# Batch 0's q in two loads of two heads, on two queues, and a new written order

## The chip, the cores and the metric

The kernel runs on one core of a Trainium2 chip. The metric is the time of one execution on the device in microseconds (us). It was measured in three runs before the change. One further execution was taken by the profiler, and all rows shown come from it.

## The reference

Softmaxed q and k, no score matrix, then a feed-forward part with a product in it. There are 8 batches, 8 heads, 576 tokens and 64 channels per head; the 4608 tokens then pass through widths 512, 1024, 1024 and 512.

```python
q_s = softmax(q, axis=-1)            # over the 64 channels, sum + 1e-9
k_s = softmax(k, axis=2)             # over the 576 tokens, sum + 1e-9
kv  = einsum('bhsd,bhse->bhde', k_s, v)
x   = einsum('bhsd,bhde->bhse', q_s, kv)   # as (4608, 512)
h   = (x @ w1) * (x @ w2) @ w3
out = h @ w_out
```

## The kernel before, in words

All inputs are float32 in memory; products run in float16. The 576 tokens of a head are laid as 64 partitions times 9 token blocks (`NJ`); two groups of four heads fill the 128 partitions. So one buffer of q for a batch is [128, 4 heads, 9 blocks, 64]. The first eight blocks of each batch make a chunk of 512 tokens for the feed-forward part; the ninth blocks of all batches make a last chunk, number 8.

The two last weights are folded first: `w3` (eight row blocks `w3.0` to `w3.7`) is turned on TensorE (`w3t`), evicted (`w3T`), multiplied by `w_out` (`wo.0`, `wo.1`) in two halves (`pf.ft.0`, `pf.ft.1`) and evicted into `W3O`. Until the first weights have landed, TensorE multiplies zeros (`zero.n`).

For each batch b, q goes through these steps in two parts p. Of the batches' q, batch 0's is turned by TensorE, the others' by a transfer.

- `qmx` (maximum, VectorE), `qsub` (subtraction, VectorE or POOL), `qexp` (ScalarE), `qsm` (sum, VectorE), `qeps` (add 1e-9), `qrc` (reciprocal, VectorE), `qn` (product, VectorE or POOL): tiles `qm`, `q`, `eq`, `qr`, `en`, lines 454 to 496.
- `qt` and `qT`: TensorE turns blocks of 128 and they are evicted, or `qd`: SP issues a transfer that turns them (line 517).
- k goes through `kmx`, `cb`, `ksub`, `kexp` (lines 362 to 414); v is cast in `vc`; `kv` and `kv2` make the 64x64 products (lines 420 to 452).
- `xm`, `xt` multiply turned q by `kv2` (line 535), evicted by `xs`, `xts` into the feed-forward's input.
- For a chunk c: `up.1` (w2), evicted by `bs`; `up.0` (w1); `ab` is their product (VectorE, line 677); `down` multiplies by `W3O` (line 684), `os` evicts, `st` stores.

The whole sequence is a written list, `ORDER`. Each engine and each queue executes its own steps in the order of that list. A suffix picks the engine (`/A` ScalarE, `/D` VectorE, `/P` POOL) or, for `zero`, the count. Steps marked `port` wait on each other when they change between VectorE and POOL (`link`). PSUM has eight banks, handed from step to step.

The inputs of batches 0 and 1 and all weights are loaded on POOL's queue, except the step in `EARLY`, which is on SP's. Loads of batches 2 to 7, the turns `qd` and the stores are on SP's queue. The first load on SP's queue that is not early waits for the third last load on POOL's (`GATE = 3`):

```python
gates[[n for n in loads if plan.steps[n]["eng"] == "SP" and n not in EARLY][0]] = [
    n for n in loads if plan.steps[n]["eng"] == "POOL"][-GATE]
```

Parts of q are cut by token blocks:

```python
PARTS = [(0, 4), (4, NJ)]
cut = slice(PARTS[name[2]][0] * D, PARTS[name[2]][1] * D)
```

Of the kernel before, what the change touches and what calls it, by code (L numbers as in the profile page):

```python
# [67 lines left out]
w3t.3 qT.0.8/A W3O.4/A w3T.3/A pf.5.1 W3O.5/A w3.0 w3t.0 w3T.0/A zero.1/1 pf.3.0 pf.3.1 W3O.3/A cb.0
ksub.0.0/D ksub.0.1/D w3.2 pf.0.0 pf.0.1 w3t.2 q.1.0 qmx.1.0 qsub.1.0/D v.0 kexp.0.0 kexp.0.1 kv.0.0 kv.0 w3.1
w3t.1 w3T.2/A pf.2.0 pf.2.1 W3O.0/A kv2.0 xm.0.0 xm.0.1 qexp.1.0 qsm.1.0 w3T.1/A pf.1.0 pf.1.1 qeps.1.0/D  # L70
xs.0.1.0/D qrc.1.0 qn.1.0/D W3O.2/A w2.2 xs.0.1.1/A up.1.0.1.2 xs.0.0.0/A xs.0.0.1/A k.1 kmx.1.0/D cb.1 w1.2
up.1.0.0.2 up.0.0.0.2 W3O.1/A up.0.0.1.2 bs.0.1.2/A ab.0.1.2 bs.0.0.2/A w2.3 up.1.0.1.3 w2.0 up.1.0.1.0
bs.0.1.0/A up.1.0.0.0 up.1.0.0.3 bs.0.0.0/A bs.0.0.3/A w2.1 up.1.0.0.1 ab.0.0.2 ksub.1.0/D bs.0.0.1/D
up.1.0.1.1 w1.0 up.0.0.1.0 up.0.0.0.0 q.1.1 qmx.1.1 bs.0.1.1/A bs.0.1.3/A ab.0.0.0 w1.1 up.0.0.0.1 w1.3
up.0.0.0.3 up.0.0.1.1 up.0.0.1.3 ab.0.1.0 ab.0.0.3 ab.0.0.1 down.0.0 v.1 ab.0.1.3 ksub.1.1/P k.2 qsub.1.1/P
kexp.1.0 kexp.1.1 qexp.1.1 qsm.1.1 vc.1.1/A os.0.0/A vc.1.0/P kv.1.0 kv.1 down.0.1 qeps.1.1/A ab.0.1.1
down.0.2 qrc.1.1 qn.1.1/P kv2.1 kmx.2.1 kmx.2.0 qd.1.0 os.0.1/A q.2 qmx.2.0 qsub.2.0/P xm.1.0 xt.0 qmx.2.1
qsub.2.1/P os.0.2/A xts.0.0/A xs.1.0.1/A xs.1.0.0/A down.0.3 os.0.3/A xts.0.1/A up.1.1.0.0 up.0.1.0.0
bs.1.0.0/A cb.2 ab.1.0.0 ksub.2.0/P st.0.0 up.1.1.0.1 bs.1.0.1/A up.0.1.0.1 up.1.1.0.2 up.0.1.0.2 v.2 qd.1.1
qexp.2.0 xm.1.1 ab.1.0.1 qsm.2.0 bs.1.0.2/A ab.1.0.2 xs.1.1.0/A xs.1.1.1/A vc.2.0/P qexp.2.1 up.1.1.0.3  # L80
up.0.1.0.3 up.1.1.1.0 qeps.2.0/A qrc.2.0 qn.2.0/P st.0.1 q.3 up.0.1.1.0 up.1.1.1.1 qsm.2.1 bs.1.0.3/A ab.1.0.3
bs.1.1.0/A kexp.2.0 qeps.2.1/A qrc.2.1 qn.2.1/P up.0.1.1.1 up.1.1.1.2 up.0.1.1.2 ksub.2.1/P up.1.1.1.3 qmx.3.1
ab.1.1.0 bs.1.1.2/A ab.1.1.2 qmx.3.0 vc.2.1/A bs.1.1.3/A bs.1.1.1/A k.3 kmx.3.1 ab.1.1.1 kexp.2.1 qsub.3.0/P
down.1.0 down.1.1 os.1.0/A os.1.1/A up.0.1.1.3 q.4 qmx.4.0 xt.1 kv.2 xts.1.0/D ab.1.1.3 qexp.3.0 qsub.4.0/P
qsub.3.1/P down.1.2 os.1.2/A qd.2.0 qd.2.1 kv2.2 xm.2.1 xts.1.1/D xs.2.1.0/A xm.2.0 xs.2.0.0/A xs.2.0.1/A
qsm.3.0 xs.2.1.1/A qeps.3.0/A kmx.3.0 qrc.3.0 qn.3.0/P down.1.3 os.1.3/A cb.3 ksub.3.1/P qexp.3.1 qsm.3.1 k.4
st.0.3 v.3 q.5 st.1.0 qd.3.0 up.1.2.0.0 bs.2.0.0/A up.0.2.0.0 up.1.2.0.1 bs.2.0.1/A up.0.2.0.1 up.1.2.0.2
up.0.2.0.2 qexp.4.0 qeps.3.1/A bs.2.0.2/A kexp.3.1 ab.2.0.1 qrc.3.1 ab.2.0.0 ksub.3.0/P kmx.4.1 kexp.3.0
st.1.1 qn.3.1/P st.0.2 st.1.2 qd.3.1 k.5 v.4 qsm.4.0 qeps.4.0/A qmx.4.1 ab.2.0.2 up.1.2.0.3 up.0.2.0.3
up.1.2.0.4 up.0.2.0.4 up.1.2.0.5 up.0.2.0.5 up.1.2.0.6 bs.2.0.5/A bs.2.0.3/A ab.2.0.3 bs.2.0.4/A bs.2.0.6/A  # L90
ab.2.0.5 ab.2.0.4 up.0.2.0.6 ab.2.0.6 up.1.2.0.7 up.0.2.0.7 vc.3.0/A bs.2.0.7/A qmx.5.1 st.1.3 vc.3.1/P v.5
kv.3 ab.2.0.7 down.2.0 kv2.3 xm.3.1 xm.3.0 qsub.4.1/P qexp.4.1 qsm.4.1 xs.3.1.0/D qrc.4.0 os.2.0/A xt.2
xs.3.0.0/A down.2.1 qsub.5.1/P xs.3.0.1/A xs.3.1.1/A down.2.2 os.2.2/A xts.2.1/A kmx.4.0 q.6 qeps.4.1/D st.2.2
qrc.4.1 down.2.3 up.1.3.0.0 cb.4 os.2.3/A bs.3.0.0/A os.2.1/D xts.2.0/A up.0.3.0.0 qn.4.1/P ksub.4.1/P
up.1.3.0.1 qexp.5.1 bs.3.0.1/A vc.4.0/P kmx.5.1 kexp.4.1 ab.3.0.0 ksub.4.0/P kmx.5.0 up.0.3.0.1 up.1.3.0.2
ab.3.0.1 bs.3.0.2/A vc.4.1/A up.0.3.0.2 up.1.3.0.3 up.0.3.0.3 qmx.5.0 ab.3.0.2 cb.5 st.2.3 qsub.5.0/P qd.4.1
kexp.4.0 qsm.5.1 up.1.3.0.4 bs.3.0.4/A up.0.3.0.4 up.1.3.0.5 bs.3.0.3/A bs.3.0.5/A k.6 qn.4.0/P qd.4.0 st.2.0
ab.3.0.3 ab.3.0.4 up.0.3.0.5 ab.3.0.5 up.1.3.0.6 up.0.3.0.6 vc.5.0/A bs.3.0.6/A up.1.3.0.7 bs.3.0.7/A
ksub.5.1/P kexp.5.1 up.0.3.0.7 xt.3 kv.4 ab.3.0.6 qexp.5.0 qeps.5.1/A ksub.5.0/P v.6 ab.3.0.7 down.3.0
down.3.1 kexp.5.0 os.3.0/A k.7 xts.3.0/A os.3.1/A kmx.6.1 kv2.4 xts.3.1/A down.3.2 qrc.5.1 qmx.6.0 xm.4.0  # L100
os.3.2/A q.7 st.2.1 xs.4.0.0/A xm.4.1 xs.4.0.1/A vc.5.1/P kv.5 qsub.6.0/P qn.5.1/P down.3.3 kmx.6.0 cb.6
ksub.6.1/D kv2.5 xs.4.1.1/A xs.4.1.0/A up.1.4.0.0 up.0.4.0.0 bs.4.0.0/A up.1.4.0.1 st.3.0 qd.5.1 v.7 os.3.3/A
st.3.3 st.3.2 vc.6.1/A bs.4.0.1/A up.0.4.0.1 up.1.4.0.2 ksub.6.0/P ab.4.0.0 qsm.5.0 qmx.6.1 up.0.4.0.2
up.1.4.0.3 up.0.4.0.3 bs.4.0.2/A kexp.6.1 bs.4.0.3/D ab.4.0.2 qeps.5.0/A qrc.5.0 ab.4.0.1 qn.5.0/P qd.5.0
ab.4.0.3 up.1.4.0.4 bs.4.0.4/A up.0.4.0.4 up.1.4.0.5 up.0.4.0.5 up.1.4.0.6 bs.4.0.5/D qexp.6.0 ab.4.0.5
qsm.6.0 ab.4.0.4 qeps.6.0/D bs.4.0.6/A up.0.4.0.6 ab.4.0.6 qrc.6.0 qn.6.0/P qsub.6.1/P up.1.4.0.7 bs.4.0.7/A
up.0.4.0.7 ab.4.0.7 down.4.0 down.4.1 down.4.2 os.4.0/A kexp.6.0 qexp.6.1 kmx.7.1 qmx.7.0 st.3.1 qmx.7.1
os.4.1/D os.4.2/A xt.4 xts.4.1/D xts.4.0/A st.4.0 qd.6.0 vc.6.0/P xm.5.0 kv.6 xm.5.1 kv2.6 qsub.7.0/P
xs.5.0.0/A xs.5.0.1/A xs.5.1.1/A down.4.3 os.4.3/A qsub.7.1/P xs.5.1.0/D up.1.5.0.0 up.0.5.0.0 qsm.6.1
qeps.6.1/D qrc.6.1 kmx.7.0 qn.6.1/P bs.5.0.0/D ab.5.0.0 qd.6.1 st.4.1 st.4.2 vc.7.0/A up.1.5.0.1 up.0.5.0.1  # L110
cb.7 up.1.5.0.2 bs.5.0.2/A up.0.5.0.2 ab.5.0.2 bs.5.0.1/A ab.5.0.1 up.1.5.0.3 ksub.7.1/P bs.5.0.3/A qexp.7.1
up.0.5.0.3 up.1.5.0.4 up.0.5.0.4 up.1.5.0.5 bs.5.0.5/A up.0.5.0.5 qexp.7.0 qsm.7.1 qeps.7.1/A ab.5.0.3
ab.5.0.5 bs.5.0.4/D ab.5.0.4 kexp.7.1 up.1.5.0.6 bs.5.0.6/A vc.7.1/P up.0.5.0.6 ab.5.0.6 qrc.7.1 ksub.7.0/P
kexp.7.0 up.1.5.0.7 bs.5.0.7/D up.0.5.0.7 ab.5.0.7 down.5.0 os.5.0/A xt.5 xts.5.0/A xts.5.1/D xm.6.0
xs.6.0.0/D xs.6.0.1/A qn.7.1/P kv.7 xm.6.1 xt.6 kv2.7 qsm.7.0 down.5.1 down.5.2 down.5.3 qeps.7.0/D qrc.7.0
xs.6.1.1/D xts.6.0/D os.5.2/A os.5.1/A xts.6.1/D xs.6.1.0/D qn.7.0/D st.5.0 qd.7.1 up.1.6.0.0 bs.6.0.0/A
up.0.6.0.0 up.1.6.0.1 bs.6.0.1/A ab.6.0.0 up.0.6.0.1 ab.6.0.1 up.1.6.0.2 bs.6.0.2/D os.5.3/A qd.7.0 xm.7.0
# [688 lines left out]
```

## Time and profile before

| | |
|---|---|
| median of 3 runs | 237.85 us (237.82 to 239.56) |
| the profiled execution | 238.41 us, of it 236.6 us from its first to its last instruction (the span) |
| granted TensorE clock | 1.0 |
| TensorE busy | 228.1 us, 96% |
| VectorE, ScalarE, POOL busy | 183.4, 118.8, 110.3 us |
| moved by transfers | 46.84 MB, mean 198 GB/s over the span |

In the profile PE is TensorE's multiplication, PEld its weight loading, DVE VectorE, ACT ScalarE, POOL GpSimd, SP SyncE. A row names line, engine, operation, the tiles written and read, shapes, count; then busy time and the idle time before, with what ended it. Times in the timeline count from the span's start. A matmul that follows another closely is counted with its pipelined end, so TensorE's busy time is not time at its peak. `w<-in_moe_w_dram` at line 294 is a load of w3, w2sb and w1sb those of w2 and w1. A step's name does not stand in a row; it is found by line, tile and place in the order.

### The profile page before, as it was taken

What the parts mean: (1) busy time and instruction counts of PE and PEld (TensorE: products, weight loads), DVE (VectorE), ACT (ScalarE), POOL (GpSimd) and SP (SyncE); (2) the same over time, 40 slices, a digit from 0 to 9 for tenths busy, and PEclk for the clock granted to TensorE, in tenths of its full rate; (3) what the DMA queues carried; (4) which work ended last, traced back from release to release, by engine and by line L of the source; (5) the groups of instructions that cost most, each with busy time, mean ns of one, the idle gap of its engine ahead of it and who ended that gap; (6) DMA issues with size and microseconds to landing.
All of it is one profiled execution on the core that took longest, in us unless ns stands there. A gap on an engine that the chain in (4) does not pass through costs nothing.

```text
span 236.6 us, 4815 instructions
## 1 busy us (share of the span) xinstructions
PE 228.1 (96%) x1930; PEld 120.6 (51%) x1930; DVE 183.4 (77%) x306; ACT 118.8 (50%) x185; POOL 110.3 (47%) x76
## 2 busy tenths in 40 slices
...
GB/s 152 260 275 279 227 285 253 328 184 390 291 393 175 351 282 253 308 402 297 290 312 379 307 146 70 24 142 3 100 178 47 0 3 0 133 9 143 72 44 133
DMA packets 39926, 46.84 MB, mean 198 GB/s; under 512 B 18400, under 2 KB 23776, under 8 KB 39904
## 3 DMA queue, kind: packets, MB, share of 16 engines
...
q8 instruction: 15, 0.25, 0.4%
...
## 4 chain that ended last, share of the span: by engine, by line
PE 81%; DMA 14%; POOL 2%; DVE 1%; issue 1%; ACT 0%; ACTq 0%; DVEq 0%; POOLq 0%
PE pab L662 51%; PE po L684 21%; DMA v<-in_v_dram 5%; DMA w<-in_moe_w_dram 5%; DMA qT<-en 4%; PE po L699 3%; PE pkv L430 2%; PE xm L535 2%; PE pf L334 2%; POOL en L494 1%; DVE qr L476 1%; DVE ab L677 1%; POOL wosb L294 0%; PE xt L535 0%; POOL q L294 0%
## 5 line engine op out<-in xcount | busy, mean ns | idle before, releaser
L662 PE MATMUL pab<-x,w1sb 128*128 128x512 f16 (+1 forms) x320 | 64.9, 336 | 0.0
L662 PE MATMUL pab<-x,w2sb 128*128 128x512 f16 (+1 forms) x320 | 64.9, 336 | 0.0
L677 DVE TENSOR_TENSOR ab<-pab,bsb 128x512 f16<-128x512 f32 x72 | 47.5, 682 | 14.8 <-PE pab L662 13.8
L684 PE MATMUL po<-W3O,ab 128*128 128x512 f16 x256 | 58.5, 379 | 0.0
L217 ACT CAST bsb<-pab 128x512 f16<-128x512 f32 x54 | 30.9, 586 | 50.2 <-PE pab L662 42.9
L662 PEld LDWEIGHTS <-w2sb 128*128 128x128 f16 x352 | 34.3, 98 | 28.5 <-issue 0.2
L662 PEld LDWEIGHTS <-w1sb 128*128 128x128 f16 x352 | 34.3, 98 | 27.9
L684 PEld LDWEIGHTS <-ab 128*128 128x128 f16 x256 | 24.2, 98 | 28.6 <-issue 0.6
L404 POOL TENSOR_TENSOR k<-k,cb 128x1152 f32<-128x1152 f32 x12 | 31.5, 2631 | 10.9 <-DVE k L404 5.8
L217 ACT COPY osb<-po 128x512 f32<-128x512 f32 (+1 forms) x28 | 15.9, 578 | 40.4 <-PE po L684 28.5
L494 POOL TENSOR_TENSOR en<-eq,qr 128x1280 f16<-128x1280 f16 (+1 forms) x12 | 25.9, 2160 | 15.1 <-DVE qr L487 12.1
L463 POOL TENSOR_TENSOR q<-q,qm 128x1280 f32<-128x1280 f32 (+1 forms) x13 | 27.7, 2141 | 8.7 <-DVE qm L458 8.7
L365 DVE TENSOR_REDUCE km<-k 128x128 f32<-128x1152 f32 x14 | 30.4, 2179 | 0.8 <-DMA k<-in_k_dram 0.8
L217 DVE CAST bsb<-pab 128x512 f16<-128x512 f32 x18 | 12.3, 682 | 16.4 <-PE pab L662 16.2
L458 DVE TENSOR_REDUCE qm<-q 128x16 f32<-128x1024 f32 (+1 forms) x16 | 21.3, 1340 | 4.3 <-DMA q<-in_q_dram 4.3
L471 ACT ACTIVATE eq<-q 128x1024 f16<-128x1024 f32 (+1 forms) x16 | 18.7, 1168 | 11.3 <-DVE q L463 7.8
L476 DVE TENSOR_REDUCE qr<-eq 128x16 f32<-128x1024 f16 (+1 forms) x16 | 21.4, 1335 | 0.5 <-ACT eq L471 0.5
L412 ACT ACTIVATE ek<-k 128x1152 f16<-128x1152 f32 x16 | 18.4, 1165 | 6.5 <-POOL k L404 6.3
L334 PE MATMUL pf<-wosb,w3T 128*128 128x512 f16 x64 | 15.0, 379 | 1.5 <-DMA wosb<-in_moe_w_out_dram 1.5
L221 ACT ACTIVATE x<-xm 128x512 f16<-128x512 f32 x24 | 12.7, 606 | 1.4 <-PE xm L535 1.4
L217 DVE COPY osb<-po 128x512 f32<-128x512 f32 (+1 forms) x9 | 5.9, 654 | 6.7 <-PE po L684 2.8
L243 PE MATMUL zero<-zero 128*128 128x512 f16 x28 | 8.9, 460 | 1.5 <-DVE zero L237 1.5
...
## 6 DMA issues: line engine op xcount, KB each, us to landing
...
k<-in_k_dram SPq DMA_DIRECT2D x6, 1152.0 KB, 6.7
q<-in_q_dram SPq DMA_DIRECT2D x6, 1152.0 KB, 8.7
v<-in_v_dram SPq DMA_DIRECT2D x6, 1152.0 KB, 9.2
...
q<-in_q_dram POOLq DMA_DIRECT2D x2, 640.0 KB, 9.7
...
k<-in_k_dram POOLq DMA_DIRECT2D x1, 1152.0 KB, 14.7
```

The lines of the kernel that those rows point to most:

```text
L217: return [(nc.scalar.copy if eng == "ACT" else engine[eng].tensor_copy)(out=out, in_=in_)]
L334: nc.tensor.matmul(st["pf", ft], lhsT=st["w3T", ft][:, gt, :], rhs=wosb[:, gt, :], start=(gt == 0), stop=(gt == N_FT - 1))
L365: dve.tensor_reduce(out=st["km", b][:, two(hp), :], in_=kb[:, two(hp), :, :].rearrange("p h j d -> p h d j"), axis=AX.X, op=ALU.max)
L404: return [engine[eng].tensor_tensor(out=kb[:, two(hp), :, :], in0=kb[:, two(hp), :, :], in1=st["cb", b][:, two(hp), None, :].broadcast_to( ...
L458: dve.tensor_reduce(out=st["qm", b][:, :, j], in_=qb[:, :, j, :], axis=AX.X, op=ALU.max)
L463: return [engine[eng].tensor_tensor(out=qb[:, :, j, :], in0=qb[:, :, j, :], in1=st["qm", b][:, :, j, None].broadcast_to([P, HH, n, D]), op ...
L471: nc.scalar.activation(out=st["eq", b, p], in_=qb[:, :, j, :], func=AF.Exp)
L476: dve.tensor_reduce(out=st["qr", b][:, :, slice(*PARTS[p])], in_=st["eq", b, p], axis=AX.X, op=ALU.add)
L494: return [engine[eng].tensor_tensor(out=st["en", b][:, j, :, :].rearrange("p j h d -> p h j d"), in0=st["eq", b, p], in1=st["qr", b][:, :, ...
L662: nc.tensor.matmul(st["p", one, c, sub, u][:, a * (t1 - t0):(a + 1) * (t1 - t0)], lhsT=w[:, ct, fb * P:(fb + 1) * P], rhs=x()[:, ct, t0:t1 ...
L677: dve.tensor_tensor(out=st["ab", c][:, nf * u:nf * u + nf, t0:t1], in0=cut(st["p", 0, c, sub, u]), in1=cut(st["bsb", c, sub, u]), op=ALU.mult)
L684: nc.tensor.matmul(st["po", c, tb], lhsT=st["ab", c][:, ft, tb * P:(tb + 1) * P], rhs=W3O[:, ft, :], start=(ft == 0), stop=(ft == N_FT - 1))
```

## The change

Batch 0 (`QH = [0]`) has its q cut by head pairs. Each of the two loads takes two heads of each group with all nine blocks, in rows of 2304 bytes (before: rows of 1024 and 1280 bytes). The first is issued on SP's queue, the second on ScalarE's queue, both ahead of everything else there; ScalarE's table load comes right after its issue. All steps of batch 0's q work on 1152 elements of each partition in both parts. The turn by TensorE is cut into four pieces by head pair and block range instead of three.

```diff
-EARLY = [("q", 0, 0)]
+EARLY = [("q", 0, 0), ("q", 0, 1)]
+BYACT = [("q", 0, 1)]
...
+    QH = [0]
...
-            if n == "k":
+            if n == "k" or i in QH:
                 heads = slice(2 * name[2], 2 * name[2] + 2)
...
-            st[name] = (nc.sync if queue == "SP" else g_).dma_start(out=dst, in_=src)
+            st[name] = {"SP": nc.sync, "ACT": nc.scalar, "POOL": g_}[queue].dma_start(out=dst, in_=src)
+            if name in BYACT[-1:]:
+                table()
...
-        load(name, "SP" if name in EARLY else "POOL")
+        load(name, "ACT" if name in BYACT else "SP" if name in EARLY else "POOL")
...
+        def part(p):
+            if b in QH:
+                return slice(2 * p, 2 * p + 2), slice(0, NJ)
+            return slice(0, HH), slice(*PARTS[p])
...
+        def qth(p, j0, j1):
+            st["qtp", b, p, j0] = bank([P, j1 - j0, P], F16, "qtp")
+            for j in range(j0, j1):
+                n = j * NHP + p
+                nc.tensor.transpose(st["qtp", b, p, j0][:, j - j0, :], blocks(st["en", b], n, n + 1),
+                                    ident16)
```

The list `ORDER` is new from its first step to its last. Its opening, and the stretch about batch 1's q:

```diff
-zero.3/3 zero.4/6 q.0.0 qmx.0.0 qsub.0.0/D w3.6 ident w3t.6 w3T.6/D zero.6/3 qexp.0.0 qsm.0.0 w3.7 w3t.7
-w3T.7/A qeps.0.0/A zero.0 q.0.1 qmx.0.1 qsub.0.1/D qexp.0.1 wo.0 pf.7.0 pf.6.0 wo.1 pf.7.1 pf.6.1 qrc.0.0
+zero.6/1 zero.3/1 q.0.0 qmx.0.0 qsub.0.0/D q.0.1 qmx.0.1 ident w3.7 qexp.0.0 qsm.0.0 zero.1/6 zero.5/1 zero.0
+zero.2/1 w3.4 w3t.4 w3T.4/A qsub.0.1/D qexp.0.1 qeps.0.0/D qrc.0.0 qn.0.0/D w3t.7 w3T.7/A wo.0 pf.4.0 qt.0.0.4
+pf.7.0 qsm.0.1 qeps.0.1/D qrc.0.1 qt.0.0.0 w3.6 w3t.6 wo.1 pf.4.1 k.0.0 qn.0.1/D qT.0.0.4/A kmx.0.0 w3T.6/A
...
+ab.0.1.1 qeps.1.1/A qrc.1.1 ksub.1.1/P qn.1.0/P q.2 qmx.2.0 qmx.2.1 down.0.0 os.0.0/A kexp.1.1 down.0.1
+os.0.1/A vc.1.0/P vc.1.1/P kv.1.0 kv.1 kv2.1 down.0.2 os.0.2/A k.2 kmx.2.0 kmx.2.1 xt.0 qd.1.0 xm.1.0 cb.2
+qn.1.1/P down.0.3 st.0.0 xts.0.1/A qsub.2.0/P xs.1.0.0/A xts.0.0/A xs.1.0.1/A up.1.1.0.0 os.0.3/A up.0.1.0.0
+up.1.1.0.1 bs.1.0.0/A ab.1.0.0 qd.1.1 qsub.2.1/P qexp.2.1 ksub.2.0/P qexp.2.0 qsm.2.0 xm.1.1 up.0.1.0.1
```

On POOL's queue the loads now go w3.7, w3.4, wo.0, w3.6, wo.1, k.0.0, k.0.1, w3.5, w3.0, w3.3, w3.2, w3.1, v.0, q.1.0, w2.3, k.1, w2.2, w2.1, w1.2, q.1.1, w1.3, w1.1, w2.0, w1.0, v.1. Before, they went w3.6, w3.7, q.0.1, wo.0, wo.1, w3.4, k.0.1, w3.5, k.0.0, w3.3, w3.0, w3.2, q.1.0, v.0, w3.1, w2.2, k.1, w1.2, w2.3, w2.0, w2.1, w1.0, q.1.1, w1.1, w1.3, v.1. SP's queue goes on with q.2, k.2, the first turn of batch 1, a store and the second turn; before with k.2, the first turn, q.2, a store, v.2 and the second turn. There are 24 multiplications of zeros instead of 28. The functions for a fused exponential (`qexps`, list `FEXP`) are in the diff but the list is empty.

More of the change, by code (lines that the diff above doesn't have):

```diff
@@ L68 @@
[L68 to L117, printed above, removed]
@@ new lines @@
+pf.7.0 qsm.0.1 qeps.0.1/D qrc.0.1 qt.0.0.0 w3.6 w3t.6 wo.1 pf.4.1 k.0.0 qn.0.1/D qT.0.0.4/A kmx.0.0 w3T.6/A
+pf.7.1 W3O.7/A qT.0.0.0/A W3O.4/A k.0.1 kmx.0.1 cb.0 ksub.0.0/D qt.0.1.4 qt.0.1.0 pf.6.0 zero.4/1 w3.5 w3t.5
+qT.0.1.0/A qT.0.1.4/A w3T.5/A pf.6.1 W3O.6/A w3.0 w3t.0 pf.5.0 pf.5.1 w3.3 w3T.0/A pf.0.0 w3t.3 pf.0.1 W3O.5/A
+kexp.0.0 w3.2 w3t.2 w3.1 w3t.1 v.0 q.1.0 w2.3 w3T.3/D pf.3.0 pf.3.1 w3T.1/A ksub.0.1/D kexp.0.1 k.1 W3O.0/A
+kv.0.0 qmx.1.0 kv.0 kv2.0 pf.1.0 pf.1.1 w2.2 w2.1 w3T.2/A W3O.3/A qsub.1.0/D xm.0.1 xm.0.0 xs.0.0.0/D
@@ new lines @@
+bs.2.0.6/A vc.3.0/A kmx.4.1 ab.2.0.5 v.4 st.0.2 ab.2.0.6 qn.3.0/P st.1.2 qd.3.1 st.0.3 vc.4.1/P qn.4.1/P
+qsub.4.0/P kv.3 bs.2.0.7/A ab.2.0.7 down.2.0 kv2.3 xt.2 xts.2.0/A os.2.0/A qd.3.0 cb.4 qmx.5.1 xm.3.1 xm.3.0
+xs.3.0.1/D down.2.1 xts.2.1/A xs.3.1.1/A xs.3.1.0/A qexp.4.0 qsm.4.0 k.5 kmx.5.1 st.1.0 v.5 down.2.2 down.2.3
+q.6 vc.4.0/A xs.3.0.0/A qeps.4.0/A qrc.4.0 os.2.1/A os.2.3/A up.1.3.0.0 up.0.3.0.0 bs.3.0.0/D qmx.5.0 ab.3.0.0
+ksub.4.1/P kmx.5.0 cb.5 qsub.5.1/P qd.4.1 st.1.3 v.6 st.2.1 qn.4.0/P ksub.4.0/P up.1.3.0.1 up.0.3.0.1 os.2.2/A
```

161 lines of the change are left out of this document (118 added, 43 removed).

## The prediction

> **What bounds the kernel now.** I read the shares of the engines first, then TensorE's waits, the stages, the chain that ended last, and the timeline of the first 64 us. From the page and from the view of TensorE's waits:
>
> ```profile
> PE 228.1 (96%) x1930; PEld 120.6 (51%) x1930; DVE 183.4 (77%) x306; ACT 118.8 (50%) x185; POOL 110.3 (47%) x76
> ...
> PE zero L243 <- DVE zero L237: 1.5, 1, 1.5
> PE pf L334 <- DMA wosb<-in_moe_w_out_dram: 1.5, 2, 0.9
> PE xm L535 <- DMA qT<-en: 1.0, 1, 1.0
> PE pkv L430 <- DMA v<-in_v_dram: 0.7, 1, 0.7
> PE w3t L324 <- DMA w<-in_moe_w_dram: 0.7, 2, 0.4
> ```
>
> TensorE is busy for 228.1 of 236.6 us. It waits 5.4 us in all, 3.9 us of that for transfers, and the latest of these waits (1.0, for the turned q of batch 1) is over by 63 us. The stage from 80 to 100 us says the same, and it names the engine that comes second (columns: stretch, length, then busy us and count of PE, PEld, DVE, ACT, POOL, the granted clock, DMA share, GB/s):
>
> ```profile
> 80.00:100.00 20.00, 20.00 (x175) 9.25 (x174) 19.75 (x33) 15.39 (x25) 15.76 (x8) 1.00 1.07 295
> ```
>
> After 63 us TensorE has no wait left to save, so a new order can only lose there. Whatever can be won lies before that: the waits for transfers, and some of the filler matmuls. VectorE has 0.25 us free in 80 to 100 us, so it is the engine that would make TensorE wait first. The transfers are saturated there too (share above 1).
>
> The opening and the first batches, from the chain that ended last (start, length) and the timeline:
>
> ```profile
> 15.97 12.36 DMA v<-in_v_dram
> 34.64 13.99 PE pab L662 x128
> 54.04 8.99 DMA qT<-en
> 63.07 0.41 PE xm L535 x8
> 75.77 0.18 PE xt L535 x8
> 75.96 0.67 PE pkv L430 x72
> 80.84 13.81 PE pab L662 x64
> ...
> 4.62 1.22 DVE L458 TENSOR_REDUCE qm<-q 128x16 f32<-128x1024 f32 x1 [3.13 <-DMA q<-in_q_dram]
> 9.61 1.49 DVE L458 TENSOR_REDUCE qm<-q 128x20 f32<-128x1280 f32 x1 [0.16 <-DMA q<-in_q_dram]
> 12.54 0.25 DVE L487 RECIPROCAL qr<-qr 128x16 f32<-128x16 f32 x1
> 12.82 1.23 DVE L494 TENSOR_TENSOR en<-eq,qr 128x1024 f16<-128x1024 f16 x1
> 15.48 0.18 DVE L483 TENSOR_SCALAR qr<-qr 128x20 f32<-128x20 f32 x1
> 16.01 1.49 DVE L494 TENSOR_TENSOR en<-eq,qr 128x1280 f16<-128x1280 f16 x1
> 12.04 1.89 PE L334 MATMUL pf<-wosb,w3T 128*128 128x512 f16 x8 [0.95 <-DMA wosb<-in_moe_w_out_dram]
> 16.19 0.66 PE L324 MATMUL w3t<-ident,w 128*128 128x128 f16 x8
> 34.48 1.91 PE L662 MATMUL pab<-x,w2sb 128*128 128x256 f16 x16
> 48.45 1.89 PE L684 MATMUL po<-W3O,ab 128*128 128x512 f16 x8
> ```
>
> VectorE works through batch 0's softmax from 4.62 to 17.50 with almost no gap. TensorE starts the first up product at 34.48 and the first down product at 48.45.
>
> **The change part by part: the loads.** The four heads of q were cut by token block (512 KB on SP's queue at once, 640 KB as the third load of POOL's queue). Now each load has two heads and all nine blocks, 576 KB, issued at once on SP and on ACT. The bytes ahead of any other load hardly change. Before wo.0 stood q.0, two blocks of w3, before v.0 seven of w3, wo, k.0, and q.1.0; now v.0 has eight of w3 ahead, and q.1.0 (512 KB) behind it, a block of w3 being 512 KB too. So I let wo.0 land at about 12 (row 12.04) and v.0 at about 28.3 (15.97 + 12.36) as before: no gain. From the list of transfers in the first 10 us (KB, median us to landing):
>
> ```profile
> q<-in_q_dram SPq DMA_DIRECT2D x1, 512.0 KB, 3.9
> q<-in_q_dram POOLq DMA_DIRECT2D x1, 640.0 KB, 6.5
> ```
>
> The first q load landed at 4.6 with hardly another in flight. Let L be the landing of the first half now. Low end: ACT's load does not disturb it, 64 KB more, 4.8. High end: both halves share evenly. From 4.6 to 9.6 (3.07, its issue, plus 6.5) came 640 KB of q and two w3 blocks that are 1 MB in memory, 1.66 MB in 5 us; the missing 640 KB of q.0 then cost 2.0 us, 6.6. Issued in the same instant, they share; I take 5.8, past the middle of that interval. [...]
>
> **VectorE and TensorE up to the first up.** VectorE has the same elements as before in equal halves of 1152, priced between 1.22 and 1.49: 1.35 each. Its order until the first half is done is maximum, subtraction, maximum of the second, sum, subtraction of the second, epsilon 0.18, reciprocal 0.26, product: 6 x 1.35 + 0.44 = 8.55, with gaps 8.8. So en's first half is ready at L + 8.8 = 14.6 (before: 14.05). TensorE's turn of it stands behind pf.4.0, and all other folds stand behind that turn. From there the same kinds of work follow as before from 16.19 to 34.48 (18.29 us): six w3 turns, 18 turns of q, kv, xm. The differences: 0.65 wait for v gone under later folds, two fillers fewer, three fold halves more (12 matmuls). A 512-column matmul is 13.81 / 64 = 0.216. So 18.29 - 0.65 - 0.43 + 2.59 = 19.8, and the first up stands at 34.4, against 34.48. The four fillers saved are no gain by themselves: 23 of 24 now run at the start, where TensorE would wait for w3 anyway.
>
> **Chunk 0.** Up products take 14.0 (row 34.64), so TensorE would be ready for the first down product at 48.4. VectorE is later. Its stretch here, by these rows:
>
> ```profile
> 34.87 1.22 DVE L372 TENSOR_TENSOR kmx<-k 128x1024 f32<-128x1024 f32 x1
> 39.60 0.45 DVE L400 STREAM_TRANSPOSE cb<-mxe 128x256 f32<-128x256 f32 x1
> 42.54 0.69 DVE L217 CAST bsb<-pab 128x512 f16<-128x512 f32 x1
> 43.15 1.48 DVE L458 TENSOR_REDUCE qm<-q 128x20 f32<-128x1280 f32 x1
> 46.97 1.29 DVE L677 TENSOR_TENSOR ab<-pab,bsb 128x512 f16<-128x512 f32 x2 [0.46 <-PE pab L662]
> ```
>
> xm ends at 34.4 - 1.73 = 32.7 and two evictions of 0.69 to 34.1. Then kmx.1.0 and cb.1 5.2, three bs 2.1, qmx.1.1 1.5, qsm.1.0 1.2, a reciprocal 0.25, seven ab 4.5: 14.7, gaps 0.5, end 49.3. The last of them, ab.0.0.0, is what the first down product reads first. In the old order it was done early. So down.0.0 starts at 49.3, +0.85.
>
> **Batch 1's q, the step that decides.** Its normalisation moves from VectorE to POOL, behind two subtractions of k and one of q; and SP's queue, held until the third last load of POOL has landed, now issues q.2 and k.2 ahead of the turn, where it had k.2 alone. The rows (SP's, then those of POOL and of the waits; after them, from the transfers issued in 40 to 50 us):
>
> ```profile
> 44.05 0.39 SPq L294 DMA_DIRECT2D k<-in_k_dram  x1
> 44.48 3.29 SPq L517 DMA_TRANSPOSE qT<-en  x1
> 47.88 0.52 SPq L294 DMA_DIRECT2D q<-in_q_dram  x1
> 42.56 2.62 POOL L404 TENSOR_TENSOR k<-k,cb 128x1152 f32<-128x1152 f32 x1 [5.76 <-DVE k L404]
> 45.15 2.33 POOL L463 TENSOR_TENSOR q<-q,qm 128x1280 f32<-128x1280 f32 x1
> 48.40 1.14 POOL L217 CAST v<-v 128x1152 f16<-128x1152 f32 x1 [0.92 <-DMA v<-in_v_dram]
> 53.05 4.25 DVE L365 TENSOR_REDUCE km<-k 128x128 f32<-128x1152 f32 x2 [0.65 <-DMA k<-in_k_dram]
> ...
> q<-in_q_dram SPq DMA_DIRECT2D x1, 1152.0 KB, 10.4
> qT<-en SPq DMA_TRANSPOSE x1, 9.4
> ```
>
> Before: k.2 issued at 44.05 held VectorE until 53.05, the turn behind it landed at 53.9 (44.48 + 9.4), the next load at 58.3 (47.88 + 10.4). They land in the order of issue, 0.9 for a turn, up to 4.4 for a load of 1.15 MB; at the 295 GB/s of 80 to 100 us a load takes 4.0. The gate opens at the same time, as the bytes through the third last load are the same. POOL's product: cb.1 ends at 39.3, then 2.6 + 2.3 + 2.6 to 46.9, reciprocal at 47.2, product 1.9 (the 2.33 of the 1280-element subtraction, scaled to 1024): 49.1. That is before the loads ahead have landed, so the queue decides, not POOL. Low end: both loads drain by 54 (53.05 plus little), turn at 54.5. High end: q.2 at 53.05, k.2 4.4 later, turn 1.1: 58.5. I take q.2 at 52.1, a little before k.2's 53.05 as no turn is issued beside it, then 4.0 + 0.9: 57. A second step gives nearly the same: VectorE now has qmx.2.0 and qmx.2.1 (2.7) ahead of kv2.1 (0.9); with q.2 landing at 52.1 to 53.05, kv2.1 ends at 55.7 to 56.6, and xm.1.0 needs it. I take 56.8. TensorE gets there at 49.3 + three down products 5.2 + kv 0.67 + xt 0.18 = 55.4: a wait of 1.4.
>
> **The sum.** From xm.1.0 the new order has 0.41, a down product 1.73 and three ups 2.6 before xm.1.1, which the old order had at 63.07 after six ups. At equal work the old one stood at 63.07 - 2.6 = 60.5; the new one at 56.8 + 4.74 = 61.5. That is +1.0. Batch 1's second turn has only small stores ahead and lands by then. POOL is some 5 us earlier with batch 2 than before; VectorE has fewer moves (two bs, one subtraction of k, one xs, one xts and three epsilons leave it, two os come): I cost the rest at nothing, its cover being these two, and the last down products, evictions and stores end in the same forms. The profiled execution, 238.41 with its span of 236.6, would become 239.4; the median shown is 0.56 lower, so 238.8.
>
> **The rivals.** *The turn of batch 1 far behind* (slower): place SP's queue at 44 us, price one us for each us after 55.7. At the high end, 58.5, it is +2.8, 240.6; from 58.1 on it decides for over 1%. For it: the 8.99 of the row at 54.04, with loads ahead. Against: v.1 is in by 48.4 (row 48.40) and leaves the engines free. *Waits removed* (faster): L near 4.8 and both loads drained by 54.5. Then VectorE runs 1 us earlier, xm.1.0 starts at 54.4, and 54.4 - 55.7 is -1.3: 236.5. For it: v.1 had landed by 48.4, and then the two loads have the engines alone. Against: kv2.1 behind q.2's landing. *VectorE as the bound* (later): with 0.25 us free in 20, a start 1.5 us later at 56 is not made up until 120 us; two waits of 0.7 at xm.2 and xm.3 more: 240.1. Against: batch 2's first ab comes at about 63.5 in both. *The change doesn't do what it says*: q.0.1 lands 3 us earlier, but VectorE's order is full, so it wins nothing at 14.6. That stands in the sum.
>
> **How the numbers follow.** The forecast 0.5, the late turn 0.25, the waits removed 0.15, VectorE 0.1. A measurement of this kernel can tell about 1% from no change (2.4 us). The slower side over 1%: most of the late turn and some of VectorE, 0.27. Faster by over 1% needs more than the whole faster rival: 0.07. The range goes from the faster rival to the late turn with some of VectorE's waits, 236.4 to 241.5.
>
> **What would show it.** Right: maximum of q at 5 to 6.6, first up at 34 to 35, down.0.0 held by ab until about 49.3, xm.1.0 waiting at about 56 to 57 for the turn or for kv2.1, no wait of TensorE after 66. Wrong: first up before 33.5 or after 36, xm.1.0 without a wait, or waits behind VectorE in 70 to 120 us.

## The result, and the profile after

The changed kernel takes 239.31 us (median of 20 runs, 237.72 to 240.45), the kernel before 237.76 in the same runs (20, 236.48 to 240.21): a ratio of 1.0075, 95% interval 1.0056 to 1.0094. It is slower by 1.55 us, inside the 1% that counts as no change, and inside the range forecast. The profiled execution took 239.29, its span is 237.5. The forecast of 238.8 is 0.5 away, but for a reason that the forecast does not contain, as the profile shows.

From the page of the changed kernel: the busy times, and of the 40 slices the granted TensorE clock. Then the view of TensorE's waits.

```profile
PE 228.5 (96%) x1926; PEld 120.0 (51%) x1926; DVE 180.3 (76%) x299; ACT 118.5 (50%) x191; POOL 113.8 (48%) x77
...
PEclk9979999999999999999999999999999999999999
...
PE qtp L552 <- DVE en L527: 2.1, 1, 2.1
...
PE pf L344 <- DMA wosb<-in_moe_w_out_dram: 1.3, 1, 1.3
PE po L745 <- DVE ab L738: 0.4, 1, 0.4
```

Two things are new. The third slice of the clock row (12 to 18 us) has a 7, where the page before has 9 throughout. And the view has no row for a turned q any more (the rows left out are `zero` at the start as before, and two of 0.4 and 0.3 for the eviction and the load of w3); TensorE's longest wait, 2.1 us, is for VectorE's en in the opening. The opening, TensorE's timeline and then the stretch from 8.5 us to the first turn (columns as in the prediction: length, busy us and count of PE, PEld, DVE, ACT, POOL, the clock, DMA share, GB/s) and two stretches of one microsecond:

```profile
11.07 1.02 PE L344 MATMUL pf<-wosb,w3T 128*128 128x512 f16 x4 [1.33 <-DMA wosb<-in_moe_w_out_dram]
14.14 0.45 PE L552 MATMUL qtp<-ident,en 128*128 128x128 f16 x5 [2.05 <-DVE en L527]
16.87 2.69 PE L344 MATMUL pf<-wosb,w3T 128*128 128x512 f16 x8
...
8.50:14.14 5.64, 2.23 (x20) 1.39 (x21) 5.57 (x7) 3.85 (x4) 1.59 (x3) 1.00 1.06 214
...
15.00:16.00 1.00, 1.00 (x7) 0.56 (x5) 0.90 (x4) 0.32 (x1) 0.65 (x1) 0.53 1.03 424
16.00:17.00 1.00, 1.00 (x12) 1.00 (x10) 1.00 (x1) 0.00 (x0) 0.59 (x1) 0.50 1.06 376
```

TensorE is busy for 2.23 of 5.64 us before the first turn, with idle times of 1.33 and 2.05 us. Then it works without a gap, but from about 15 us the granted clock is 0.50, and eight fold matmuls that take 1.89 us elsewhere take 2.69. By 19 us it is 1.00 again. What comes of it stands in the chain that ended last and in the timeline around batch 1's q:

```profile
35.80 13.97 PE pab L723 x128
81.01 13.81 PE pab L723 x64
...
49.69 3.63 PE L745 MATMUL po<-W3O,ab 128*128 128x512 f16 x16
55.92 0.39 PE L579 MATMUL xm<-qT,kv 64*64 64x256 f16 x8
60.70 0.41 PE L579 MATMUL xm<-qT,kv 64*64 64x256 f16 x8
```

The first up product starts at 35.80 (before 34.64, 1.16 later), but batch 1's second xm (60.70, where the prediction puts the kernel before at 60.5 for equal work) and the start of chunk 2 (81.01 against 80.84) are only 0.2 us behind. So a loss in the opening stands against a gain of about 1 us before 63 us, where the kernel before waited for the turned q. The runs of the changed kernel say the same of the clock. Three have a mean clock of 0.998 or more and a median of 237.92, eight have 0.992 or 0.993 and 239.2, nine have 0.983 to 0.986 and 239.95. The profiled execution is one of the eight, so what the nine lost besides stands in no trace.

### The profile page after: what moved, and what is told of

It reads as the page before. It is cut to its first block, busy times and chain, and to the rows that moved or that the text cites. A ratio compares the mean times of both kernels' runs of the same rounds, so it can differ in the third digit from the quotient of the medians.

```text
span 237.5 us, 4816 instructions
## 1 busy us (share of the span) xinstructions
PE 228.5 (96%) x1926; PEld 120.0 (51%) x1926; DVE 180.3 (76%) x299; ACT 118.5 (50%) x191; POOL 113.8 (48%) x77
## 3 DMA queue, kind: packets, MB, share of 16 engines
q0 software_dynamic: 7312, 10.55, 19.9%
## 4 chain that ended last, share of the span: by engine, by line
PE 89%; DVE 5%; DMA 2%; ACT 2%; issue 1%; DVEq 0%; ACTq 0%
PE pab L723 52%; PE po L745 23%; PE pf L344 5%; PE po L760 3%; PE pkv L440 2%; DMA q<-in_q_dram 2%; PE xm L579 2%; DVE qm L477 1%; DVE q L483 1%; PE w3t L334 1%; ACT w3T L220 1%; DVE ab L738 1%; DVE en L527 1%; DVE qr L509 1%; ACT W3O L224 0%
## 5 line engine op out<-in xcount | busy, mean ns | idle before, releaser
L723 PEld LDWEIGHTS <-w2sb 128*128 128x128 f16 x352 | 34.4, 98 | 28.1
L414 POOL TENSOR_TENSOR k<-k,cb 128x1152 f32<-128x1152 f32 x13 | 34.0, 2625 | 13.8 <-DVE cb L410 10.9
L527 POOL TENSOR_TENSOR en<-eq,qr 128x1280 f16<-128x1280 f16 (+1 forms) x13 | 27.8, 2140 | 12.8 <-DVE qr L520 11.4
L477 DVE TENSOR_REDUCE qm<-q 128x16 f32<-128x1024 f32 (+2 forms) x16 | 21.2, 1332 | 4.4 <-DMA q<-in_q_dram 4.4
L491 ACT ACTIVATE eq<-q 128x1024 f16<-128x1024 f32 (+2 forms) x16 | 18.6, 1172 | 7.6 <-DVE q L483 7.5
L220 DVE COPY osb<-po 128x512 f32<-128x512 f32 (+1 forms) x11 | 7.2, 665 | 19.9 <-PE po L745 13.4
L509 DVE TENSOR_REDUCE qr<-eq 128x16 f32<-128x1024 f16 (+2 forms) x16 | 21.5, 1341 | 0.1
L344 PE MATMUL pf<-wosb,w3T 128*128 128x512 f16 x64 | 16.6, 400 | 1.7 <-DMA wosb<-in_moe_w_out_dram 1.3
L224 ACT ACTIVATE x<-xm 128x512 f16<-128x512 f32 x25 | 13.9, 608 | 0.6 <-PE xm L579 0.6
L220 DVE CAST bsb<-pab 128x512 f16<-128x512 f32 x16 | 10.8, 681 | 4.1 <-PE pab L723 4.0
L344 PEld LDWEIGHTS <-w3T 128*128 128x128 f16 x64 | 5.9, 102 | 8.0 <-ACT w3T L220 1.9
```

What stands on the lines that cost most here:

```text
L220: return [(nc.scalar.copy if eng == "ACT" else engine[eng].tensor_copy)(out=out, in_=in_)]
L344: nc.tensor.matmul(st["pf", ft], lhsT=st["w3T", ft][:, gt, :], rhs=wosb[:, gt, :], start=(gt == 0), stop=(gt == N_FT - 1))
L414: return [engine[eng].tensor_tensor(out=kb[:, two(hp), :, :], in0=kb[:, two(hp), :, :], in1=st["cb", b][:, two(hp), None, :].broadcast_to( ...
L477: dve.tensor_reduce(out=st["qm", b][:, hs, j], in_=qb[:, hs, j, :], axis=AX.X, op=ALU.max, **({"negate": True} if (b, p) in FEXP else {}))
L491: nc.scalar.activation(out=st["eq", b, p], in_=qb[:, hs, j, :], func=AF.Exp)
L509: dve.tensor_reduce(out=st["qr", b][(slice(None), *part(p))], in_=st["eq", b, p], axis=AX.X, op=ALU.add)
```

## The experiments

The theory after this reading: the change costs 1.6 us because TensorE's idle time in the opening lets the clock fall, and the order itself is as good as the one before. The rivals: the loads (the ACT queue, the row size), the order on SP's queue, VectorE. Times are medians, the kernel before measured beside each group in brackets. The groups ran on different chips. By the ratios only e4 and e13 stand more than 1% from the kernel before; the smaller differences below are read within a group and from the traces.

| run | time | ratio to before, 95% interval | mean clock of the runs |
|---|---|---|---|
| e7, three fillers moved | 237.75 (237.35) | 1.0014, 0.9996 to 1.0032 | 0.998 to 1.00, one of 12 at 0.993 |
| e1, 15 fillers in the opening | 237.73 (237.43) | 0.9998, 0.9973 to 1.0022 | 0.998 to 1.00 |
| e3, before with fillers moved away | 237.75 (237.43) | 1.001, 0.9981 to 1.0039 | 10 of 12 under 0.994 |
| e2, both halves on SP's queue | 237.46 (237.43) | 0.9991, 0.997 to 1.0013 | 1.00, three at 0.993 |
| e12, before with both parts on SP's queue | 238.11 (237.55) | 1.0012, 0.9989 to 1.0034 | 0.993 to 1.00 |
| e13, second half late on POOL's queue | 239.78 (237.55) | 1.0108, 1.0085 to 1.0131 | 0.986 to 0.993 |
| e4, q of batch 2 behind the turn | 241.86 (237.43) | 1.0176, 1.0138 to 1.0213 | 0.993 to 1.00 |
| e10, k of batch 2 behind the turn | 239.21 (237.42) | 1.0077, 1.0054 to 1.01 | 1.00 |
| e9, before with the turn ahead of v | 237.45 (237.35) | 1.0011, 0.9992 to 1.003 | 0.998 to 1.00 |
| e6, e1 with ab ahead of ksub | 237.11 (237.35) | 0.9999, 0.9988 to 1.0011 | 0.998 to 1.00 |
| e5, three edits together | 236.72 (237.35) | 0.9981, 0.9965 to 0.9997 | 0.998 to 1.00 |
| e11, e5 again | 236.87 (237.42) | 0.997, 0.995 to 0.999 | 0.999 to 1.00 |

**The clock: e1, e7 and e3.** First the idle times filled with 15 fillers (the changed kernel has 24 in all, e1 has 36; the one behind `pf.6.0` moves too):

```diff
-... zero.1/6 zero.5/1 zero.0
-zero.2/1 w3.4 ... wo.0 pf.4.0 qt.0.0.4
+... zero.1/6 zero.0
+w3.4 ... wo.0 zero.5/6 pf.4.0 zero.2/6 zero.4/3 qt.0.0.4
```

> The changed kernel with its fillers (multiplications of zeros) laid elsewhere: 21 at the start instead of 23, six ahead of the first fold half, nine ahead of the first turn of q, none later. Theory A (the clock): the changed kernel loses its time because TensorE is idle too long between 8.5 and 14.1 us (busy 2.23 of 5.64), whereupon its clock is granted at half for about 3.4 us. With the fillers the clock stays at 1.0, the folds from 14.5 to 18.6 shrink from 0.43 to 0.22 us a matmul, the first up moves from 35.8 to about 34.3 to 34.8, and the median falls from 239.3 to 237.4 to 238.0. Rival B (the wait for batch 1's turned q and the product behind it, as predicted): this is at 50 to 57 us and untouched, the median stays at 239 to 239.5. Rival C (VectorE): also untouched, VectorE holds the first down product at about 49.3, the median stays within 0.5 us of 239.3.

237.73, all 12 runs within 0.25 us, against 239.31. Then the smaller dose, which moves three fillers and adds no instruction: `wo.0 zero.5/1 pf.4.0 zero.2/1 zero.4/1 qt.0.0.4`.

> The same kernel with 3 fillers in the place of the 15 (one ahead of pf.4.0, two ahead of the first turn): TensorE is then busy for about 2.9 of the 5.64 us from 8.5 to 14.14, against 2.23 with the clock drop and 5.41 without it, and its idle times are about 1.1 and 1.6 us. If the clock falls by the share of busy time, and 51% is enough (59% was enough with q on SP's queue alone), 237.7 and a clock of 1.00. If the clock falls wherever one idle time is well over a microsecond, 239.3 and 0.99. If the moved fillers won for some other reason than the clock, such as the turn of q standing later in TensorE's order, the time is near 237.7 with a clock still at 0.99.

237.75. Three matmuls of 0.22 us, placed in the idle time, are worth 1.56 us against the changed kernel's 239.31. Measured from the kernel before of each group it is 1.15 (0.40 above it instead of 1.55), and in the traces the first up moves by 1.60. Stretch and timeline of e7, its first up and its two xm:

```profile
8.50:14.14 5.64, 3.08 (x25) 1.66 (x23) 5.57 (x7) 3.95 (x4) 1.67 (x4) 1.00 1.07 214
...
14.17 0.45 PE L552 MATMUL qtp<-ident,en 128*128 128x128 f16 x5 [1.27 <-DVE en L527]
16.08 1.89 PE L344 MATMUL pf<-wosb,w3T 128*128 128x512 f16 x8
54.34 0.39 PE L579 MATMUL xm<-qT,kv 64*64 64x256 f16 x8
59.12 0.41 PE L579 MATMUL xm<-qT,kv 64*64 64x256 f16 x8
...
34.20 13.97 PE pab L723 x128
79.43 13.81 PE pab L723 x64
```

The first turn stands where it stood (14.17 against 14.14), so VectorE and the first half's load did not move; the eight folds are back at 1.89, and everything from the first up on is 1.6 us earlier. The counterpart takes fillers out of the idle time of the kernel before: `zero.0`, 13 matmuls, moves to the start, and the 12 of `zero.3`, `zero.4` and `zero.6` shrink to 3.

> The kernel before with its 13 fillers moved from the wait at 8 to 11 us to the start, and three groups at one each in place of 3, 6 and 3: TensorE is then idle from about 8.2 to 12.0 except for one w3 turn. Theory A: the clock drops at about 12 to 14 us here too, its mean over the span is 0.985 to 0.993, and the median rises by 1 to 2 us over the kernel before, to 238.8 to 239.8. Rivals B and C: fillers are no work, the first up stays at 34.5 and the median within 0.4 us of the kernel before.

```profile
12.07 5.30 PE L334 MATMUL pf<-wosb,w3T 128*128 128x512 f16 x16 [3.32 <-DMA wosb<-in_moe_w_out_dram]
28.37 0.48 PE L430 MATMUL pkv<-v,ek 64*64 64x64 f16 x36
34.48 1.69 PE L662 MATMUL pab<-x,w2sb 128*128 128x256 f16 x14
...
13.00:14.00 1.00, 1.00 (x4) 0.45 (x3) 1.00 (x1) 1.00 (x1) 0.00 (x0) 0.50 1.08 203
```

The clock fell there too, but the time did not change (237.75 against 237.43, the interval holds 1): that expectation of a loss was a miss. The second and third row say why: the first kv stands at 28.37 and the first up at 34.48, to the hundredth where the kernel before had them. That one waited 0.65 us for v at this place; here the slow folds use up that wait, and nothing is lost behind it. So in these kernels half a clock is paid for only where the work behind it is TensorE's own, as in the new order.

**The loads: e2, e12 and e13.** The empty list `BYACT = []` puts both halves on SP's queue.

> The changed kernel with both loads of batch 0's q on SP's queue, one behind the other; nothing else moved. In the changed kernel the two queues shared the engines and the halves landed at 5.68 and 6.03. Theory A: the first half lands at 4.8 to 5.0, VectorE's chain and the first turn of q come 0.7 to 0.9 us earlier (13.3 instead of 14.1), TensorE's idle stretch is shorter by as much, and the clock drops in fewer executions: median 238.0 to 239.0. Rival B (the wait at batch 1's turn decides): no change, 239 to 239.5. Rival D (the second queue is worth something): the second half lands 0.3 us or more later than 6.03 and VectorE waits for it; median the same or up to 0.5 us more.

237.46, better than the 238.0 to 239.0 expected: this removes the loss as well, in another way. With both loads on one queue VectorE's maximum of the first half starts at 4.45 instead of 5.71, en comes 1.26 us earlier, and the idle time before the turn shrinks from 2.05 to 0.89:

```profile
12.88 0.45 PE L552 MATMUL qtp<-ident,en 128*128 128x128 f16 x5 [0.89 <-DVE en L527]
```

Three of its 12 runs have a clock of 0.993, and at 237.45 to 237.80 they are no longer than the others; no trace shows where their clock fell.

In the changed kernel the later loads landed about 1 us earlier than before (by POOL's next issue behind them, wo.0 at 11.21 against 12.28, v.0 at 27.65 against 28.61), which the prediction did not have. Two runs tell whether the rows of 2304 bytes or the early issue did it: the kernel before with its narrow rows and both parts early (`EARLY = [("q", 0, 0), ("q", 0, 1)]`), and e7 with its wide rows, the second half's load third on POOL's queue and VectorE's maximum of that half put behind it.

> The kernel before, with its cut of q by token block (rows of 1024 and 1280 bytes) and its order, and only the second part's load (640 KB) moved from third on POOL's queue to second on SP's, issued at about 1.2 us. In the changed kernel the first fold weights landed 1.06 us earlier than before and the transfers from 3 to 5 us ran at 395 GB/s instead of 296. If the early issue on a second, otherwise idle queue does that, this kernel shows about 390 there and wo.0 near 11, v.0 near 27.4. If the wider rows of 2304 bytes do it, about 300, and wo.0 stays near 12. The time by either: 237.4 within 0.5, since TensorE waits for v and for the turned q of batch 1 later.

> The counterpart: the changed kernel with the three fillers in the opening (237.75), the halves cut by heads with rows of 2304 bytes, and only the second half's load put third on POOL's queue as in the kernel before. If the early issue made the loads quick, the transfers from 3 to 5 us fall to about 300 GB/s and wo.0 lands near 12; if the rows did, they stay near 390 and wo.0 near 11. VectorE's maximum of the second half then starts at about 9.5 instead of 8.5, behind the sum of the first, which costs the first half of en nothing; the time is 237.7 to 238.3.

The stretch from 3 to 5 us in the kernel before, the changed one, e12 and e13 (the last number is GB/s), then e13's first fold and the fillers behind e12's first turn of w3:

```profile
3.00:5.00 2.00, 2.00 (x7) 0.60 (x4) 0.38 (x1) 0.00 (x0) 2.00 (x5) 1.00 1.14 296
3.00:5.00 2.00, 2.00 (x7) 0.70 (x5) 0.00 (x0) 0.00 (x0) 2.00 (x5) 1.00 1.01 395
3.00:5.00 2.00, 2.00 (x7) 0.60 (x4) 0.30 (x1) 0.00 (x0) 2.00 (x5) 1.00 1.07 385
3.00:5.00 2.00, 2.00 (x7) 0.65 (x5) 0.72 (x1) 0.00 (x0) 2.00 (x4) 1.00 0.83 181
...
12.96 1.75 PE L344 MATMUL pf<-wosb,w3T 128*128 128x512 f16 x4 [2.48 <-DMA wosb<-in_moe_w_out_dram]
...
8.45 1.48 PE L243 MATMUL zero<-zero 128*128 128x512 f16 x3
```

Early issue gives 385 to 395 GB/s with either rows, late issue 296 and 181, so in this stretch the gain goes with the early issue. The rows count ahead of it: from 1.7 to 3 us the kernels with wide rows moved 183 to 259 GB/s (the changed one 183, e2 220, e13 259), those with narrow rows 111 and 123 (e12, before). In e12 the first fold stands behind fillers at 14.70 without a wait, so its row does not show when wo.0 landed; how the 1.07 us of the changed kernel divide between the early issue, the rows and the new order stays open, as does why e13, with the same bytes ahead as the kernel before, is the slowest.

Both times were misses. In e13 wo.0 lands so late that TensorE idles 2.48 us, the clock falls again (0.50 from 14 to 16 us), and it takes 239.78. In e12 the early q delays the first block of w3, TensorE's fillers run out and it idles 2.01 us. Behind that it works more slowly: its first eight turns take 1.07 us (0.71 in the kernel before, where they stood at 5.86), three fillers 1.48 (0.81) and the next 13 take 4.28 (2.97). The clock column shows 1.00 there all the same, as it does in the kernel before while its first nine fillers take 4.02. The first up starts at 35.55 in the chain (34.64 in the kernel before); the median is 238.11, though the interval holds 1.

**SP's queue: e4, e10 and e9.** The forecast made the two loads ahead of batch 1's turn its main cost. e4 (on top of e1) puts `q.2 qmx.2.0 qmx.2.1` behind `qd.1.0`, e10 (on top of e5) puts `k.2 kmx.2.0 kmx.2.1` behind it.

> The fillers as in the first run, and batch 2's q load put behind batch 1's first turn on SP's queue, as in the kernel before (k.2, turn, q.2); VectorE's two maxima of q.2 then come behind kv2.1 and batch 2's maxima of k. Theory A: in the changed kernel xm.1.0 did not wait for the turn (it starts at 55.92 right behind xt), so this moves the median by no more than 0.4 us against the first run; 237.2 to 238.2. Rival B (the loads ahead of the turn cost time): 0.7 to 1.5 us less than the first run.

> The best version so far (236.72; one profiled run of it at 237.77) with the load of k of batch 2 and its two maxima behind the first turn of batch 1's q on SP's queue, q of batch 2 staying ahead. In the profiled run that turn landed at 54.9, behind k at 53.9, and the first xm of batch 1 waited 0.43 us for it; VectorE's kv2 of batch 1 was done at 54.36. If the turn behind k is the wait, it lands by about 52.5, xm starts at 54.6 without a wait, and the slower runs go: 236.6, all within 0.4 us. If k of batch 2 is needed as early as q of batch 2 (whose delay cost 4 us), VectorE's maxima of k start about a microsecond later, the subtraction, the exponential and the kv of batch 2 follow, and the time goes to 237.5 or more.

Both are far slower, e4 by 4.1 us than e1, which was expected to be no more than 0.4 away, e10 by 2.3 than e5's second measurement (e11) in the same group. From e4, ScalarE's and TensorE's timeline, and from e10, VectorE's:

```profile
63.15 2.22 ACT L491 ACTIVATE eq<-q 128x1280 f16<-128x1280 f32 x2 [5.00 <-POOL q L483]
66.88 1.23 PE L723 MATMUL pab<-x,w2sb 128*128 128x256 f16 x8 [2.10 <-ACT x L224]
...
68.00:69.00 1.00, 1.00 (x7) 0.67 (x6) 1.00 (x3) 1.00 (x3) 0.36 (x2) 0.50 1.08 401
```

```profile
56.16 4.28 DVE L375 TENSOR_REDUCE km<-k 128x128 f32<-128x1152 f32 x2 [2.60 <-DMA k<-in_k_dram]
```

The load that was moved is issued 7.3 us later in e4 (49.73 against 42.42 in the changed kernel) and lands 3 us later in e10 (56.1 against 53.2 in the changed kernel), and the engines work in list order: in e10 VectorE stands 2.60 us before its maxima, in e4 they start at 57.64 behind those of k, POOL's subtraction follows at 58.92, ScalarE waits 5.00 us for it with batch 1's x queued behind, and TensorE waits 2.10 for that x. In e4 the clock too falls behind this idle time, in the middle of the kernel (0.50 from 68 to 71 us); its runs at 0.993 are about 1 us above those at 1.00 (242.2 to 242.6, and 241.3 to 241.6). So q.2 and k.2 ahead of the turn are a gain of this order, not its cost.

The other way round, in the kernel before: where does its wait of 1.0 at 63 us come from? `v.2 qd.1.1` becomes `qd.1.1 v.2`.

> The kernel before with one step moved: the load of v of batch 2 behind the second turn of batch 1's q on SP's queue. If the wait of 1.0 us at 63 us comes from the load ahead of that turn (it landed at 61.9, the turn at 63.0), the turn lands by about 59.5, the wait is gone, and the time goes to 236.8; and if that load's landing is what makes the kernel before vary from 236.6 to 239.7, its runs draw together to within some 0.5 us. If the turn only waits for q of batch 2 (landed 58.3) it is still rid of the 1.0. If the 1.0 is taken back elsewhere, by v of batch 2 or by VectorE, 237.4 and the same spread.

```profile
61.42 0.41 PE L535 MATMUL xm<-qT,kv 64*64 64x256 f16 x8
96.62 0.63 PE L535 MATMUL xm<-qT,kv 64*64 64x512 f16 x8 [1.07 <-issue]
```

The wait at 63 us is gone (61.42 instead of 63.07; 0.6 of the difference was there at the first up), and 1.07 us of waiting comes back at 96.62, ahead of batch 3's xm; its row names nothing that ended it. The time is unchanged, and so is the spread: this load is not what makes the kernel before vary by 3 us from run to run. What does stays open.

**The end: e6, and all together: e5 and e11.** The order of the changed kernel has `ksub.7.0/D` ahead of `ab.5.0.7`; e6 swaps them, on top of e1.

> The kernel with the fillers moved into the opening (237.73), and besides it VectorE's last subtraction of k (batch 7) is put behind ab.5.0.7. If that subtraction (2.39 us) is what holds down.5.0 for 0.4 us at 162 us, TensorE loses that wait, the span goes from 235.8 to 235.4 and the time to 237.3. If the wait merely moves (batch 7's k comes 0.7 us later to TensorE's kv.7, or another eviction is late), 237.7 as before the edit.

237.11, so 0.62 less than e1. In its own group it is 0.64 less than e7, and its longest run (237.50) is below e7's shortest (237.55); the ratios to the kernel before, whose runs spread over more than 2 us, don't show it. The wait of down.5.0 for ab is gone and no other takes its place. e5 has e6's swap, `BYACT = []`, and 7 fillers (`wo.0 zero.5/3 pf.4.0 zero.2/3 zero.4/1 qt.0.0.4`).

> Three edits together: both halves of q on SP's queue, 7 fillers in TensorE's idle times of the opening (3 ahead of pf.4.0, 4 ahead of the first turn), and VectorE's last subtraction of k behind ab.5.0.7. If the clock, the later landing of the first half and the wait at 162 us are separate losses, first up at about 33.1 and the time 237.46 minus 0.4, 237.0 or a little under, with a clock of 1.00 in all runs. If the start of chunk 0 is bound by weights that land later (a wait of 0.2 for w2 was there with q on SP alone), the gain of the opening ends there and the time stays at 237.4.

> The best version once more, beside the run above on the same chip, so that its trace in its more frequent time (236.6) can be set beside the trace at 237.77. If the difference of 1.1 us lies in the landing of the weights and of k of batch 1 (TensorE waited 0.8 for w3, POOL 2.49 us for an issue), the first up stands at about 33.1 and xm of batch 1 at 54 without a wait. If it lies behind 66 us, both traces agree until there.

236.72 and 236.87: less than both kernels, than the kernel before by 0.2 to 0.3%, with intervals that stay below 1, though a difference of this size still counts as no change. Two of 12 and one of 12 runs took 237.75 to 238.01, the first profiled one among them. The chains of the slower (e5) and the usual execution (e11):

```profile
19.60 14.74 DMA k<-in_k_dram
49.01 5.88 DMA qT<-en
55.02 0.41 PE xm L579 x8
...
47.78 6.10 DMA qT<-en
54.01 0.41 PE xm L579 x8
```

k of batch 1 landed at 34.34 in the slower one, VectorE's maxima started behind it at 34.36 (33.21 in the other), POOL's product and the turn followed, and xm is 1.0 us later. Behind the opening, the turn that stands behind both loads is the one thing that TensorE still waits for: 0.43 and 0.31 us.

## Why the prediction was right in size and wrong in cause

The stretch from chunk 5's first up to TensorE's last matmul, of before and of after, and VectorE in the changed kernel ahead of ab.5.0.7; then its rows, and those of SP's queue, that answer to the prediction's steps:

```profile
148.39:233.46 85.07, 85.06 (x505) 39.45 (x502) 48.94 (x85) 22.99 (x39) 12.10 (x6) 1.00 0.31 66
148.57:234.41 85.84, 85.43 (x505) 39.35 (x502) 45.14 (x76) 22.50 (x41) 7.93 (x4) 1.00 0.31 69
...
161.98 2.39 DVE L414 TENSOR_TENSOR k<-k,cb 128x1152 f32<-128x1152 f32 x1
...
5.71 1.35 DVE L477 TENSOR_REDUCE qm<-q 128x18 f32<-128x1152 f32 x1 [4.21 <-DMA q<-in_q_dram]
12.72 1.36 DVE L527 TENSOR_TENSOR en<-eq,qr 128x1152 f16<-128x1152 f16 x1
35.21 1.22 DVE L382 TENSOR_TENSOR kmx<-k 128x1024 f32<-128x1024 f32 x1
44.98 1.88 DVE L738 TENSOR_TENSOR ab<-pab,bsb 128x512 f16<-128x512 f32 x3
47.53 2.11 DVE L738 TENSOR_TENSOR ab<-pab,bsb 128x512 f16<-128x512 f32 x3
42.42 0.39 SPq L302 DMA_DIRECT2D q<-in_q_dram  x1
42.91 1.17 SPq L302 DMA_DIRECT2D k<-in_k_dram  x1
...
q<-in_q_dram SPq DMA_DIRECT2D x1, 1152.0 KB, 7.8
k<-in_k_dram SPq DMA_DIRECT2D x1, 1152.0 KB, 10.3
```

In the account of the profiled executions the kernel before took 238.41. At full clock the change gains 1.4 up to the second xm of batch 1 (59.12 in e7, where equal work before stood at 60.5): 0.44 at the first up (34.20 against 34.64) and the wait of 0.98 for the turned q. It loses 0.77 at the end (85.84 against 85.07, with 0.41 of it the wait for ab), and the clock costs 1.6: 239.4, measured 239.29. The kernel before was profiled 0.65 above its median, which makes the 1.55 between the medians.

- *The first half's landing, 5.8, and en at 14.6.* Right for the landing: VectorE's maximum starts at 5.71. The chain from there to en takes 8.4 and not 8.8, so en is done at 14.09. Sharing between the two queues is what the traces show: with a half on each (the changed kernel) they landed at 5.68 and 6.03 and the maximum of the first started at 5.71, with both on SP's queue (e2) it started at 4.45. The high end of 6.6, the estimate for even sharing, was not reached.
- *wo.0 and v.0 as before, "no gain".* Wrong by 1 us: 10.9 and 27.4. Bytes ahead were counted, not how early and how fast they move: 395 GB/s against 296 from 3 to 5 us.
- *First up at 34.4.* The sum of 19.8 from en to first up was right at full clock (e7: 14.13 to 34.04 in the timeline, 19.9). In the changed kernel it took 21.5. The step that failed is this: every duration in it was a row at full clock, and "the four fillers saved are no gain by themselves" left out what fillers are for. The place of three of them decides 1.6 us: first up at 35.64 in the timeline that the prediction reads, 35.80 in the chain.
- *First down held by VectorE until 49.3.* Mis-sized: from kmx.1.0 to the last of the needed ab it took 14.4 us (35.21 to 49.64) and not 15.2, because successive products overlap a little (three ab in 1.88, with a mean of 0.680 for one; I counted 0.645 each and gaps). VectorE was ready 0.14 us ahead of TensorE's 49.78, and no wait stands there.
- *The turn of batch 1 at 57, a wait of 1.4.* Wrong in size: q.2 landed at 50.2 (42.42 + 7.8) and k.2 at 53.2 (42.91 + 10.3). I took 4.0 us for a load, from the 295 GB/s of a later stage; here k.2 came 3.0 us behind q.2. And the gate opened at 42.42 and not at 44.05. The earlier landing of the loads (v.0 by 1 us) explains about 1 us of that; the rest is not followed up. The low end (54.5) was the good one: e11's turn landed at 53.9.
- *The rest at nothing.* One term was there: a wait of 0.4 us for ab.5.0.7 inside down.5.0, up to 165.03, behind the subtraction that starts at 161.98. With what follows it was worth 0.62.

So errors cancelled, and the size came out by luck. The sum had batch 1's second xm at 61.5; at full clock it comes at 59.12, 2.4 earlier. Against that stand 1.6 for the clock and 0.8 for the end, and neither was in the sum. The prediction's own sign of being wrong came too: xm.1.0 started without a wait. The faster rival (waits removed, xm.1.0 at 54.4) describes what this order does at full clock to 0.1 us (54.34), though its landing near 4.8 did not come; its 236.5 was not reached because of the end and because the profile of before stood above its median.
